# A gated token mixer built from 26-product block schemes: one product as seven sub-products, PSUM in pairs of banks, and another order of the stages

## The chip, the cores and the metric

One Trainium2 chip, one core. The metric is the device time of one execution in microseconds (us); the median of three runs is given. TensorE is called PE, VectorE DVE, ScalarE ACT, GpSimd POOL and SyncE SP. POOL and SP issue the DMAs.

## The reference

All is f32: x is 2048 x 1024 (S x D), the MLP works along S with F = 3584. The Fourier branch is the real part of the two-dimensional DFT, by DFT matrices. The other branch is a layer norm and an MLP across tokens.

```
a = x @ hid_re.T ; b = x @ hid_im.T
y = seq_re @ a - seq_im @ b                  # branch A, S x D
h = layernorm(x)                             # over D
u = gelu(w1.T @ h + b1)                      # F x D
o = w2.T @ u + b2                            # branch B, S x D
g = sigmoid(sum over D of x * gate_w)        # one number per row
out = g * y + (1 - g) * o
```

## The kernel before, in words

There are four matrix products, each a stage (a class derived from `Bilinear`): `Fourier` (q, the sequence DFT of x), `Mixed` (y, the hidden DFT of q), `Up` (u) and `Down` (o). Each stage cuts its two operands into 4 x 4 and 4 x 2 blocks, and computes the block product by a bilinear scheme with 26 block products where the plain way takes 32. An operand of product j is a sum or difference of blocks, made on DVE (`add`, `sub`; L569, L572). It is then split into a high and a low part (`split_into`): ACT writes the high part rounded to fp32r (L599), DVE the remainder (L604, L606). PE multiplies high by high, high by low and low by high (L902, L903, L904), so one 128x128x512 piece is three matmuls. In PSUM the products of the scheme are "chained" where one product can go on accumulating in the banks of the one before. Where results are due, a bank is read (evicted): copied by ACT or DVE (`plain_copy`, L938, L940) or added to a result in SBUF by DVE (`fused`, L946). Down's evictions multiply by the row's gate as well: `hgate`, `ngate` on DVE, or ACT at L1210.

The names: `q_p9` is the tenth product of stage q; `q_R...`, `q_W...` its blocks and their sums; `_r_`, `_w_` with hi and lo the split operands; `ps_o_p9_2_0` the PSUM bank for rows block 2 of o's product 9; `o_c...` a result of Down that is being summed in SBUF. `Q_TAKES = 1, 1, 2` says how many blocks of K the groups of a product take: PE works through all banks of one group before the next group.

SBUF and PSUM are divided into fixed slots: `SLOTS` has 51 full tiles of 1024 columns, and 8 PSUM tiles `ps` of one bank (512 columns). A half buffer takes half of a full tile.

No queue decides at run time. `Graph.schedule` is a list scheduler: each instruction has a cost and a due time from its `key` (a place in PE's sequence), and is written out, engine by engine, in the order that results. On each engine that order is fixed, and semaphores hold an instruction back until what it reads or overwrites is ready. PE's order is that of the stages and products.

Of the kernel before, what the change touches and what calls it, by code (L numbers as in the profile page):

```python
# [14 lines left out]
P = 128  # L15
# [3 lines left out]
H = 512  # L19
# [5 lines left out]
SLOTS = {"f": 51, "h": 1, "ps": 8}  # L25
LATE = 3.0

# [112 lines left out]
Q_GAP = 8  # L140
U_ORDER = [20, 9, 8, 19, 15, 18, 1, 16, 10, 4, 21, 22, 11, 7, 3, 17, 5, 14, 23, 6, 24, 0, 13, 12, 2, 25]
# [68 lines left out]
SUMS_AT, SUMS_STEP = ("q", 12), 2.5  # L210
SQUARES_AT, SQUARES_STEP = ("y", 6), 2
H_LEAD, H_EACH = 25, 1.3
# [49 lines left out]
class Buf:  # L262
    def __init__(self, kind, name, t=None, parts=1, dtype=F32):
        self.kind, self.name, self.t, self.parts, self.dtype = kind, name, t, parts, dtype
        self.writer = [None] * parts
        self.readers = [[] for _ in range(parts)]
        self.taker = None
        self.users, self.opens = set(), False


class View:
# [7 lines left out]
    @property  # L279
    def reg(self):  # L280
        return (self.buf, self.part)

# [19 lines left out]
class Store:  # L302


    def __init__(self, slots):
        self.free = {k: [Slot(k, i) for i in range(n)] for k, n in slots.items()}
        self.part = {F32: [], F32R: []}

    def pairs(self, ahead):
        return sum((max(0, ahead[d] - len(self.part[d])) + 1) // 2 for d in self.part)  # L310

    def fits(self, b, ahead):
        if b.kind != "h":
            return len(self.free[b.kind]) > ahead[b.kind]
        if len(self.part[b.dtype]) > ahead[b.dtype]:
            return True
        return len(self.free["f"]) + len(self.free["h"]) > ahead["f"] + self.pairs(ahead)

    def take(self, b):
        if b.kind != "h":  # L320
            b.slot = min(self.free[b.kind], key=lambda s: s.at), None
            self.free[b.kind].remove(b.slot[0])
            return
        halves = self.part[b.dtype]
        if halves:
            b.slot = min(halves, key=lambda x: x[0].at)
            halves.remove(b.slot)
        else:
            pool = self.free["h"] or self.free["f"]
            b.slot, b.opens = (min(pool, key=lambda s: s.at), 0), True  # L330
            pool.remove(b.slot[0])
            if b.slot[0].pool == "f":
                halves.append((b.slot[0], 1))
        b.slot[0].inside[b.slot[1]] = True

    def give(self, b, now):
        s, h = b.slot
        s.at = now
        if h is not None and s.pool == "f":
            s.inside[h] = False  # L340
            if s.inside[1 - h]:
                self.part[b.dtype].append(b.slot)
                return
            self.part[b.dtype].remove((s, 1 - h))
        self.free[s.pool].append(s)


class Graph:
# [63 lines left out]
    def schedule(self):  # L412
        store = Store(SLOTS)
        waiting = {k: [] for k in ("f", F32, F32R, "ps")}
# [11 lines left out]
        for t in self.tasks:  # L426
            left[t] = len(t.deps)
            for b in t.bufs:
                users[b] = len(b.users)
            for b in t.need:  # L430
                insort(waiting[b.dtype if b.kind == "h" else b.kind], t)
# [6 lines left out]
        def has_slots(t):  # L438
            if not all(b.engine for b in t.behind):
                return False  # L440
            for b in t.need:
                if not store.fits(b, {k: bisect_left(waiting[k], t) for k in waiting}):
                    return False
            return True

        def start(t, e):
            nonlocal dma
            t.engine, t.start = e, now
            order.append(t)
            for b in t.need:  # L450
                store.take(b)
                waiting[b.dtype if b.kind == "h" else b.kind].remove(t)
# [50 lines left out]
def gated_mix_kernel(  # L503
# [30 lines left out]
        "ps": (ctx.enter_context(tc.tile_pool(name="psum", bufs=1, space=bass.MemoryType.PSUM)), H),  # L534
# [138 lines left out]
    class Bilinear:  # L673
# [10 lines left out]
        behind = ()  # L684
        ahead = 3

        def __init__(self, name, nk, nm, nn, wn, rn, big, keep, order, extra, perm):
# [7 lines left out]
            self.again = {j: s for j in range(1, len(rows)) for s in (1, -1) if small[j] == [s * c for c in small[j - 1]]}  # L695
# [13 lines left out]
            for i, (w, v) in enumerate(zip(self.out, self.out[n:])):  # L709
                same = sum(a != b for a, b in zip(w, v))  # L710
                opposite = sum(a != -b for a, b in zip(w, v))
                go_on = min(same, opposite) < sum(a != 0 for a in w)
# [18 lines left out]
        def groups(self):  # L731
# [14 lines left out]
        def during(self, j, key):  # L746

            if (self.name, j) == SUMS_AT:
# [3 lines left out]
                gates(key + SUMS_STEP * NS)  # L752
            if (self.name, j) == SQUARES_AT:
                for row in range(NS):
                    row_squares(row, key + SQUARES_STEP * row)
                rstds(key + SQUARES_STEP * NS)

# [45 lines left out]
        def operand(self, x, j, k, key):  # L803
# [3 lines left out]
            for o, ((a, ca, la), (b, cb, lb)) in ops:  # L807
                if self.by_dma(x, j, k, o):
                    swap = self.fresh(x, a, k, la) is None
                    if swap:  # L810
                        (a, ca, la), (b, cb, lb) = (b, cb, lb), (a, ca, la)
                    src = self.fresh(x, a, k, la)
                    if src is not None and lb and fresh.get(b) != k and (b >= (16 if x == self.big else 8) or x not in self.resident):
                        held = (b, k) in self.val[x] or b < (16 if x == self.big else 8)
                        sb = self.val[x][b, k][1] if (b, k) in self.val[x] else self.stored.get((x, b, k), 1)
                        if held and ca * src[1] == cb * sb:
# [10 lines left out]
                            continue  # L827
                (va, sa, mine_a), (vb, sb, mine_b) = self.term(x, a, la, j, k, key), self.term(x, b, lb, j, k, key)
# [61 lines left out]
        def matmuls(self, j, ks, ops, eps):  # L890
            first, end = ks[0] == 0 and not self.chained[j], ks[-1] == self.nk - 1
            for m in range(self.nm):
                c = slice(m * P, (m + 1) * P)
                for n in range(self.nn):
                    if first:
                        self.PS[j % self.chains, m, n] = View(Buf("ps", f"ps_{self.name}_p{j}_{m}_{n}", None, 4), 0, H)
# [11 lines left out]
                    if end:  # L908
                        key = step + len(ks) + (m * self.nn + n) / (self.nm * self.nn)
                        for q, coef in self.reads[j]:  # L910
                            b = self.perm[0][q // 2] * 2 + self.perm[2][q % 2]
                            o = self.C.get((b, m, n))
                            back = self.back(b, j)
                            if o is None:
                                o = self.C[b, m, n] = self.c_slots(f"{self.name}_c{b}", b, m, n)
                                if back:
                                    self.bring(key - self.ahead, b, m, n, o)
                                    self.accumulate(key, b, m, n, o, bank, eps * coef)
                                else:
                                    self.copy(key, b, m, n, o, bank, eps * coef)  # L920
                            else:
                                self.accumulate(key, b, m, n, o, bank, eps * coef)
                            if j in self.ends[b]:
                                self.finish(key + 1, b, m, n, self.C.pop((b, m, n)), j)

        def c_slots(self, name, b, m, n):
            i = m * self.nn + n
# [22 lines left out]
    class Fourier(Bilinear):  # L950
        wide = Q_WIDE
        behind = Q_BEHIND
        gap = Q_GAP
# [4 lines left out]

        def source(self, x_, b, k):
# [3 lines left out]
            return x[i * P:(i + 1) * P, h * H:(h + 1) * H], ()  # L963

# [52 lines left out]
        def matmuls(self, j, ks, ops, eps):  # L1017
# [13 lines left out]
            if j or ks != (0,):  # L1031
                return super().matmuls(j, ks, ops, eps)
            for n in range(2):
                for m in range(4):
                    self.PS[0, m, n] = View(Buf("ps", f"ps_q_p0_{m}_{n}"), 0, H)
# [137 lines left out]
    class Down(Bilinear):  # L1173
# [5 lines left out]
        ahead = O_AHEAD  # L1179

# [82 lines left out]
    def row_sums(k, key):  # L1263
# [4 lines left out]
        g.add({"DVE": dve(D)}, key, lambda e: nc.vector.scalar_tensor_tensor(  # L1268
            v.ap, v.ap, 1.0, GW.ap, op0=ALU.mult, op1=ALU.mult, accum_out=zg.t[:, col]),
            r=(v.reg, GW.reg), w=(v.reg, zg))  # L1270

    def small(engine, key, fn, r, w, n=1):
        g.add({engine: 0.2 * n}, key, fn, r=r, w=w)

    def gates(key):
# [6 lines left out]
        def rest(e):  # L1282
# [10 lines left out]
        small("DVE", key, lambda e: nc.vector.tensor_scalar(  # L1293
            nmean.t, sums.t, -1.0 / D, None, op0=ALU.mult), (sums,), (nmean,))
# [34 lines left out]
    def normalise(k, v, key):  # L1329

        load(key, v, x[k * P:(k + 1) * P, :])
        g.add({"ACT": act(D) + 0.08}, key, lambda e: nc.scalar.activation(
# [14 lines left out]
    for st in (Fourier(), Mixed(), Up(), Down()):  # L1347
        st.build()
# [60 lines left out]
```

## Time and profile before

| | |
|---|---|
| timed runs, median of 3 | 1849.24 us (1849.2 to 1850.03) |
| span of the profiled execution | 1847.2 us |
| PE busy, matmuls | 1843.0 us, 8130 |
| DVE busy, instructions | 1692.7 us, 2372 |
| ACT busy, instructions | 876.2 us, 1311 |
| POOL busy | 207.2 us |
| granted TensorE clock | 1.000 |
| DMA | 472.71 MB, mean 256 GB/s |

The profiled execution's own time is its span, from the first instruction to the last; the device time of a run holds about 2 us more. In a group's row stand: line, engine, operation, out<-in, tile shapes, count, then busy time and mean ns of one, then the engine's idle time just ahead of them and what ended it. In a timeline row stand start and duration in us. A PE record is longer than the pitch of the matmuls, since they overlap in the pipeline.

### The profile page before, as it was taken

The page shows a single profiled execution, that of the slowest core. Times are in us where ns is not written, and L with a number is a line of the kernel's source. Part 1 is how long each engine was busy: PE and PEld are TensorE (multiplying, and loading weights), DVE is VectorE, ACT ScalarE, POOL GpSimd, SP SyncE. Part 2 cuts the span into 40 slices and gives each one's busy share as a digit, 9 for nine tenths or more (in the row PEclk, how much of TensorE's full clock was granted, in tenths as well). Part 3 has the DMA queues.
Part 4 walks back from the last instruction along what each step waited for, and adds up shares of the span by engine and source line. Part 5 has one row for each costly group of instructions (what it writes and reads, how often), then busy time and mean ns, then how long its engine had stood idle before and what let it go on. Part 6 is the DMA issues. An engine that isn't in the chain of part 4 may idle for free.

```text
span 1847.2 us, 24030 instructions
## 1 busy us (share of the span) xinstructions
PE 1843.0 (100%) x8130; PEld 1525.2 (83%) x8130; DVE 1692.7 (92%) x2372; ACT 876.2 (47%) x1311; POOL 207.2 (11%) x355
## 2 busy tenths in 40 slices
PE   9999999999999999999999999999999999999999
PEld 7888888888888888888888888888888888888887
DVE  8999679989989999999789698879999999999995
ACT  5533334534344686597343344444654534444441
POOL 0100010111021001001121000001220000001111
PEclk9999999999999999999999999999999999999999
DMA  9977377969698888988676547667899676775963
GB/s 377 368 260 270 126 280 289 349 236 376 237 333 313 303 292 273 332 312 292 219 256 241 174 136 255 225 210 247 301 365 295 193 210 208 217 215 128 301 156 69
DMA packets 189739, 472.71 MB, mean 256 GB/s; under 512 B 23152, under 2 KB 23920, under 8 KB 189616
## 3 DMA queue, kind: packets, MB, share of 16 engines
q1 hardware_dynamic: 156384, 368.40, 58.4%
q0 software_dynamic: 32944, 102.52, 16.6%
q8 instruction: 63, 1.03, 0.2%
q14 instruction: 60, 0.49, 0.1%
q10 hardware_dynamic: 288, 0.26, 0.0%
HBM read 367.29 MB, written 103.81 MB: 255 GB/s over the span
## 4 chain that ended last, share of the span: by engine, by line
PE 100%; DVE 0%; issue 0%; DVEq 0%
PE ps_q_p L902 10%; PE ps_q_p L904 10%; PE ps_q_p L903 10%; PE ps_u_p L904 9%; PE ps_u_p L902 9%; PE ps_u_p L903 9%; PE ps_o_p L902 9%; PE ps_o_p L904 9%; PE ps_o_p L903 9%; PE ps_y_p L903 5%; PE ps_y_p L904 5%; PE ps_y_p L902 5%; PE ps_q_p L1049 0%; PE ps_q_p L1026 0%; PE pw L1343 0%; DVE o_c L946 0%
## 5 line engine op out<-in xcount | busy, mean ns | idle before, releaser
L904 PE MATMUL ps_q_p<-q_p_r_hi,q_p_w_lo 128*128 128x512 f32 x728 | 283.2, 389 | 0.0
L902 PE MATMUL ps_o_p<-o_p_r,o_p_w 128*128 128x512 f32 x726 | 282.4, 389 | 0.0
L903 PE MATMUL ps_o_p<-o_p_r,o_p_w 128*128 128x512 f32 x726 | 282.4, 389 | 0.0
L904 PE MATMUL ps_o_p<-o_p_r,o_p_w 128*128 128x512 f32 x726 | 282.4, 389 | 0.0
L903 PE MATMUL ps_u_p<-u_p_r_lo,u_p_w_hi 128*128 128x512 f32 x588 | 228.7, 389 | 0.0
L902 PE MATMUL ps_q_p<-q_p_r_hi,q_p_w_lo 128*128 128x512 f32 x584 | 227.2, 389 | 0.0
L903 PE MATMUL ps_q_p<-q_p_r_lo,q_p_w_lo 128*128 128x512 f32 x584 | 227.2, 389 | 0.0
L902 PE MATMUL ps_u_p<-u_p_r_lo,u_p_w_hi 128*128 128x512 f32 x504 | 196.1, 389 | 0.0
L904 PE MATMUL ps_u_p<-u_p_r_lo,u_p_w_lo 128*128 128x512 f32 x504 | 196.1, 389 | 0.0
L599 ACT ACTIVATE q_p_r_hi<-q_R_p 128x1024 fp32r<-128x1024 f32 (+1 forms) x100 | 104.2, 1053 | 161.8 <-DVE q_R_p L569 78.7
L599 ACT ACTIVATE u_p_w_hi<-u_W_p 128x896 fp32r<-128x896 f32 x104 | 97.1, 950 | 141.1 <-DVE u_W_p L569 69.5
L904 PEld LDWEIGHTS ps_q_p<-q_p_r_hi,q_p_w_lo 128*128 128x128 f32 x728 | 136.7, 188 | 28.4
L904 PEld LDWEIGHTS ps_o_p<-o_p_r,o_p_w 128*128 128x128 f32 x726 | 136.3, 188 | 28.4
L902 PEld LDWEIGHTS ps_o_p<-o_p_r,o_p_w 128*128 128x128 f32 x726 | 136.3, 188 | 28.2
L903 PEld LDWEIGHTS ps_o_p<-o_p_r,o_p_w 128*128 128x128 f32 x726 | 136.3, 188 | 28.2
L599 ACT ACTIVATE o_p_r<-o_R_p 128x512 fp32r<-128x512 f32 x117 | 72.5, 626 | 120.9 <-PE ps_o_p L904 37.3
L903 PEld LDWEIGHTS ps_u_p<-u_p_r_lo,u_p_w_hi 128*128 128x128 f32 x588 | 110.4, 188 | 23.0
L903 PEld LDWEIGHTS ps_q_p<-q_p_r_lo,q_p_w_lo 128*128 128x128 f32 x584 | 109.6, 188 | 22.7
L902 PEld LDWEIGHTS ps_q_p<-q_p_r_hi,q_p_w_lo 128*128 128x128 f32 x584 | 109.7, 188 | 22.6
L946 DVE SCALAR_TENSOR_TENSOR q_c<-ps_q_p,q_c 128x512 f32<-128x512 f32 x168 | 110.3, 686 | 15.6 <-PE ps_q_p L904 11.5
L606 DVE TENSOR_TENSOR q_p_r_lo<-q_R_p,q_p_r_hi 128x1024 fp32r<-128x1024 f32 (+1 forms) x100 | 120.4, 1215 | 4.5 <-ACT q_p_r_hi L599 4.4
L904 PEld LDWEIGHTS ps_u_p<-u_p_r_lo,u_p_w_lo 128*128 128x128 f32 x504 | 94.6, 188 | 19.6
(322 smaller groups left out, 3989.4 us busy)
## 6 DMA issues: line engine op xcount, KB each, us to landing
q_R_p<-in_ct_dram SPq DMA_DIRECT2D x131, 512.0 KB, 7.5
u_W_p<-in_w_dram SPq DMA_DIRECT2D x120, 448.0 KB, 4.7
o_R_p<-in_w_dram SPq DMA_DIRECT2D x99, 256.0 KB, 4.7
o_R_p<-u SPq DMA_DIRECT2D x83, 256.0 KB, 5.2
q<-q_c POOLq DMA_DIRECT2D x80, 256.0 KB, 6.2
o_W_p<-in_w_dram SPq DMA_DIRECT2D x76, 256.0 KB, 4.9
q_W_p<-in_x_dram SPq DMA_DIRECT2D x75, 256.0 KB, 5.5
u<-u_c POOLq DMA_DIRECT2D x72, 256.0 KB, 4.7
```

The costliest lines, as they stand in the source:

```text
L599: g.add({"ACT": act(v.n)}, key, lambda e: nc.scalar.activation(hi.ap, v.ap, AF.Copy, scale=-1.0 if negate else 1.0), r=(v.reg,), w=(hi.reg,))
L606: nc.vector.tensor_sub(lo.ap, v.ap, hi.ap.bitcast(F32))
L902: nc.tensor.matmul(bank.ap, wh.ap[:, c], rh.ap[:, e], start=a, stop=False, skip_group_check=True)
L903: nc.tensor.matmul(bank.ap, wh.ap[:, c], rl.ap[:, e], start=False, stop=False, skip_group_check=True)
L904: nc.tensor.matmul(bank.ap, wl.ap[:, c], rh.ap[:, e], start=False, stop=b, skip_group_check=True)
L946: lambda e: nc.vector.scalar_tensor_tensor(o.ap, ps.ap, scale, o.ap, op0=ALU.mult, op1=ALU.add),
```

## The change

1. `Q_INNER = (24,)`: the scheme's row 24, which is product 9 of stage q, is done by the new function `strassen`: both operands are halved in K, rows and columns, and seven sub-products of 2 x 2 pieces are made (the variant with sums that are used again). It is 84 matmuls in place of 96. DVE makes the extra sums in SBUF, and in PSUM two sums across banks (`add(step, q12, q21, p5)` and `add(step, q22, q21, p5)`).
2. PSUM: 4 tiles `pp` of two banks take the place of 8 of one. With `together` (q, u, y) two neighbouring banks are one buffer and are evicted by one 1024-wide instruction. Down has `together = False`: its banks are single buffers, each a half of a pair tile.
3. `RESERVE = 7` bounds how many slots the planner keeps back for work that is due earlier.
4. The stages run Fourier, Up, Mixed, Down.
5. The row sums, row squares and gates, that the layer norm and the gate need, come at other places: `SUMS_AT`, `SQUARES_AT`, `GATES_AT`, and the DVE product for the gate moves into `normalise`.
6. Stage q takes K in groups of (2, 2) in place of (1, 1, 2), except in product 0, and W of two blocks of K as one 1024-wide tile.

```diff
-SLOTS = {"f": 51, "h": 1, "ps": 8}
+SLOTS = {"f": 51, "h": 1, "pp": 4}
+RESERVE = 7
+Q_INNER = (24,)
-SUMS_AT, SUMS_STEP = ("q", 12), 2.5
-SQUARES_AT, SQUARES_STEP = ("y", 6), 2
-H_LEAD, H_EACH = 25, 1.3
+SUMS_AT, SUMS_STEP = ("q", 4), 2.5
+SQUARES_AT, SQUARES_STEP = ("q", 12), 2
+GATES_AT = "u", 10
+H_LEAD, H_EACH = 8, 0.6
-Q_TAKES = 1, 1, 2
+Q_TAKES = 2, 2
-Q_WIDE, Y_WIDE, O_WIDE = "", "WR", ""
+Q_WIDE, Y_WIDE, O_WIDE = "W", "WR", ""
...
     def take(self, b):
-        if b.kind != "h":
+        if b.kind in ("f", "pp"):
...
-        halves = self.part[b.dtype]
+        halves = self.part[b.lane]
         if halves:
             b.slot = min(halves, key=lambda x: x[0].at)
             halves.remove(b.slot)
         else:
-            pool = self.free["h"] or self.free["f"]
+            pool = self.free["pp"] if b.kind == "ps" else self.free["h"] or self.free["f"]
...
-                if not store.fits(b, {k: bisect_left(waiting[k], t) for k in waiting}):
+                if not store.fits(b, {k: min(bisect_left(waiting[k], t), RESERVE) for k in waiting}):
...
-                for ks in self.groups():
+                if j in self.inner:
+                    self.strassen(j, factor)
+                    continue
+                for ks in self.groups(j):
...
+        def banks(self, j):
+            every = [(m, n) for n in range(self.nn) for m in range(self.nm)]
+            for i, (m, n) in enumerate(every):
+                name = f"ps_{self.name}_p{j}_{m}_{n}"
+                if not self.together or i == len(every) - 1 and i % 2 == 0:
+                    self.PS[j % self.chains, m, n] = View(Buf("ps", name, None, 4), 0, H)
+                elif i % 2 == 0:
+                    both = Buf("pp", name, None, 2)
+                    self.PS[j % self.chains, m, n] = View(both, 0, H, 0)
+                else:
+                    self.PS[j % self.chains, m, n] = View(both, H, H, 1)
...
+            q11, q12, q21, q22 = quarter(0, 0), quarter(0, 1), quarter(2, 0), quarter(2, 1)
+            products(folded(step, "a11", a(0, 0)), halves(step, "b11", [b(0, 0), b(1, 0)]), 2, 0, True, True)
+            step += 1
+            plain_copy(step, q11, q21, 1.0)
...
+            p5 = slot(D, f"{name}_p5")
+            plain_copy(step, p5, q22, 1.0)
...
+            products(folded(step, "s2", Fold(s)), whole(step, "t2", whole_t), 2, 0, False, True)
+            step += 1
+            add(step, q12, q21, p5)
...
+            products(folded(step, "s3", Fold(s3)), whole(step, "t3", whole_t3), 2, 0, False, True)
+            step += 1
+            add(step, q22, q21, p5)
+            ready(2, 1, step + 1)
...
     class Down(Bilinear):
+        together = False
...
-    for st in (Fourier(), Mixed(), Up(), Down()):
+    for st in (Fourier(), Up(), Mixed(), Down()):
```

What the order of instructions shows of it, at three places. A row has its number on the engine, the line, the operation, out<-in and what it waits for; a tile has the name of the buffer that first took it.

PE where Down's product 8 ends and product 9 begins, before:

```order
6703 L903 MATMUL ps_o_p_3_0_12211<-o_p_r_12433,o_p_w_12483 128x512
6704 L904 MATMUL ps_o_p_3_0_12211<-o_p_r_12433,o_p_w_12483 128x512
6705 L902 MATMUL ps_o_p_0_0_12650<-o_p_r_12523,o_p_w_12459 128x512 [waits Activation_49]
6706 L903 MATMUL ps_o_p_0_0_12650<-o_p_r_12523,o_p_w_12459 128x512 [waits DVE_49]
6707 L904 MATMUL ps_o_p_0_0_12650<-o_p_r_12523,o_p_w_12459 128x512
```

And now, PE and then DVE at the same place:

```order
6670 L950 MATMUL ps_o_p_2_0_11851<-o_p_r_12058,o_p_w_12072 128x512
6671 L948 MATMUL ps_o_p_2_0_11851<-o_p_r_12095,o_p_w_12083 128x512 [waits DVE_49,Activation_49]
6672 L949 MATMUL ps_o_p_2_0_11851<-o_p_r_12095,o_p_w_12083 128x512
6673 L950 MATMUL ps_o_p_2_0_11851<-o_p_r_12095,o_p_w_12083 128x512
6674 L948 MATMUL ps_o_p_2_0_11851<-o_p_r_12109,o_p_w_12112 128x512 [waits Activation_49]
6675 L949 MATMUL ps_o_p_2_0_11851<-o_p_r_12109,o_p_w_12112 128x512
6676 L950 MATMUL ps_o_p_2_0_11851<-o_p_r_12109,o_p_w_12112 128x512
6677 L948 MATMUL ps_o_p_2_0_11851<-o_p_r_12095,o_p_w_12083 128x512 [waits DVE_49]
```

```order
1595 L609 TENSOR_TENSOR o_W_p_3_10674<-o_W_p_3_10674 128x512 [waits DMAHW5_49,DMAHW4_49]
1596 L1016 SCALAR_TENSOR_TENSOR o_c_2_11993<-ps_o_p_2_0_11851,ngate,o_c_2_11993 128x512 [waits PE_49]
1597 L606 TENSOR_TENSOR o_W_p_2_10641<-o_W_p_3_10674,o_W_p_2_10641 128x512 [waits DVE_49]
1598 L1016 SCALAR_TENSOR_TENSOR o_c_2_11993<-ps_o_p_2_0_11851,ngate,o_c_2_11993 128x512 [waits DMAHW6_49,PE_49]
1599 L643 TENSOR_TENSOR o_p_r_12307<-u_c_6_7355,o_p_r_12307 128x512 [waits Activation_49]
```

Before, product 9 began in a bank of its own (`..._12650`) while product 8's last bank (`..._12211`) was emptied. Now the first matmul of product 9 (row 6671) writes into the tile that product 8's last matmul (row 6670) wrote into, and it waits for DVE, whose evictions of the two halves (rows 1596 and 1598) wait for PE. The second half's first matmul is row 6677.

DVE at the start, behind product 0's operands, before:

```order
12 L569 TENSOR_TENSOR q_R_p_0_277<-q_R_p_0_277,q_R_p_0_286 128x1024 [waits DMAHW4_49,DMAHW3_49]
13 L569 TENSOR_TENSOR q_R_p_0_259<-q_R_p_0_277,q_R_p_0_259 128x1024 [waits DVE_49]
14 L572 TENSOR_TENSOR q_W_p_0_311<-q_W_p_3_273,q_W_p_0_311 128x512 [waits DMAHW6_49,DMAHW5_49]
15 L940 TENSOR_SCALAR q_c_0_410<-ps_q_p_0_0_282 128x512 [waits PE_49]
16 L569 TENSOR_TENSOR q_W_p_0_257<-q_W_p_0_311,q_W_p_0_257 128x512 [waits DVE_49]
17 L606 TENSOR_TENSOR q_p_r_lo<-q_R_p_0_259,q_p_r_hi 128x1024 [waits Activation_49]
18 L569 TENSOR_TENSOR q_R_p_1_315<-q_R_p_1_315,q_R_p_1_333 128x1024 [waits DMAHW7_49,DMAHW0_49]
19 L604 SCALAR_TENSOR_TENSOR q_p_w_lo<-q_W_p_0_257,q_p_w_hi 128x512 [waits Activation_49]
```

And now:

```order
11 L606 TENSOR_TENSOR q_R_p_0_265<-q_R_p_0_265,q_R_p_0_273 128x1024 [waits DMAHW4_49,DMAHW3_49]
12 L606 TENSOR_TENSOR q_R_p_0_247<-q_R_p_0_265,q_R_p_0_247 128x1024 [waits DVE_49]
13 L606 TENSOR_TENSOR q_R_p_1_279<-q_R_p_1_279,q_R_p_1_298 128x1024 [waits DMAHW6_49,DMAHW5_49]
14 L643 TENSOR_TENSOR q_p_r_lo<-q_R_p_0_247,q_p_r_hi 128x1024 [waits Activation_49]
15 L606 TENSOR_TENSOR q_R_p_1_252<-q_R_p_1_279,q_R_p_1_252 128x1024 [waits DVE_49]
16 L609 TENSOR_TENSOR q_W_p_0_1_329<-q_W_p_0_1_302,q_W_p_0_1_329 128x1024 [waits DMAHW2_49,DMAHW7_49,DMAHW1_49,DMAHW0_49]
17 L643 TENSOR_TENSOR q_p_w_1_lo<-q_W_p_0_1_302,q_p_w_1_hi 128x1024 [waits Activation_49]
18 L606 TENSOR_TENSOR q_W_p_0_1_344<-q_W_p_0_1_329,q_W_p_0_1_344 128x1024 [waits DMAHW4_49,DMAHW3_49,DVE_49]
19 L643 TENSOR_TENSOR q_p_r_lo<-q_R_p_1_252,q_p_r_hi 128x1024 [waits Activation_49]
20 L606 TENSOR_TENSOR q_R_p_2_367<-q_R_p_2_367,q_R_p_2_371 128x1024 [waits DMAHW6_49,DMAHW5_49]
21 L641 SCALAR_TENSOR_TENSOR q_p_w_1_lo<-q_W_p_0_1_344,q_p_w_1_hi 128x1024 [waits Activation_49]
```

The first group of product 1 had its W part ready with row 19, after one block of K; now with row 21, after two, and W is summed and split 1024 columns at a time.

DVE in the last part of q's product 9, now:

```order
169 L1010 TENSOR_SCALAR q_p_p_1836<-ps_q_p_2_1_1807 128x1024 [waits DVE_49,PE_49]
170 L643 TENSOR_TENSOR q_p_t_lo<-q_p_t,q_p_t_hi 128x1024 [waits Activation_49]
171 L609 TENSOR_TENSOR q_W_p_0_1_1740<-q_W_p_0_1_1740,q_W_p_0_1_1791 128x1024 [waits DMAHW6_49,DMAHW5_49,DMAHW3_49]
172 L606 TENSOR_TENSOR ps_q_p_0_1_1860<-ps_q_p_2_0_1780,q_p_p_1836 128x1024 [waits DVE_49,PE_49]
173 L643 TENSOR_TENSOR q_p_r_lo<-q_R_p_0_1718,q_p_r_hi 128x1024 [waits Activation_49]
174 L1016 SCALAR_TENSOR_TENSOR q_c_0_761<-ps_q_p_0_0_1814,q_c_0_761 128x1024 [waits PE_49]
175 L643 TENSOR_TENSOR q_p_w_1_lo<-q_W_p_0_1_1740,q_p_w_1_hi 128x1024 [waits Activation_49]
176 L643 TENSOR_TENSOR q_p_r_lo<-q_R_p_1_1772,q_p_r_hi 128x1024 [waits Activation_49]
177 L606 TENSOR_TENSOR ps_q_p_2_1_1807<-ps_q_p_2_0_1780,q_p_p_1836 128x1024 [waits PE_49]
```

Rows 172 and 177 are the two sums in PSUM. Before, product 9 had no such rows: only its low parts and eight evictions of 512 columns.

More of the change, by code (lines that the diff above doesn't have):

```diff
@@ L684, in gated_mix_kernel @@
         behind = ()
+        halved = ()
+        together = True
         ahead = 3
@@ L694, in __init__ @@
             small = [r[1] for r in rows]
-            self.again = {j: s for j in range(1, len(rows)) for s in (1, -1) if small[j] == [s * c for c in small[j - 1]]}
+            self.inner = [j for j, r in enumerate(order) if r in self.halved]
+            self.again = {j: s for j in range(1, len(rows)) for s in (1, -1)
+                          if small[j] == [s * c for c in small[j - 1]] and not {j, j - 1} & {*self.inner}}
             self.kept = {}
@@ L711, in __init__ @@
                 opposite = sum(a != -b for a, b in zip(w, v))
-                go_on = min(same, opposite) < sum(a != 0 for a in w)
+                go_on = min(same, opposite) < sum(a != 0 for a in w) and i + n not in self.inner
                 self.chained.append(go_on)
@@ L908, in matmuls @@
                     if end:
[L909 to L924, printed above, removed]
+                        self.take(step + len(ks) + (n * self.nm + m) / (self.nm * self.nn), j, m, n, eps)
@@ new lines, in take @@
+        def take(self, key, j, m, n, eps):
+            bank, at = self.PS[j % self.chains, m, n], [(m, n)]
+            if bank.buf.kind == "pp":
+                if bank.c0 == 0:
+                    return
+                at.insert(0, (m - 1, n))
+                bank = View(bank.buf, 0, D)
+            for q, coef in self.reads[j]:
+                b = self.perm[0][q // 2] * 2 + self.perm[2][q % 2]
+                new, back = (b, m, n) not in self.C, self.back(b, j)
+                if new:
+                    for one in at:
+                        self.C[(b, *one)] = self.c_slots(f"{self.name}_c{b}", b, *one)
+                os = [self.C[(b, *one)] for one in at]
+                o = os[0] if len(at) == 1 else View(os[0].buf, 0, D)
+                if new and back:
+                    for one, part in zip(at, os):
+                        self.bring(key - self.ahead, b, *one, part)
+                if new and not back:
+                    self.copy(key, b, m, n, o, bank, eps * coef)
+                else:
+                    self.accumulate(key, b, m, n, o, bank, eps * coef)
+                if j in self.ends[b]:
+                    for one in at:
+                        self.finish(key + 1, b, *one, self.C.pop((b, *one)), j)
```

178 lines of the change are left out of this document (144 added, 34 removed).

## The prediction

> **What bounds the kernel now.** I read the page first (busy times, clock, chain), then the waits of PE, then single instructions.
>
> ```profile
> PE 1843.0 (100%) x8130; PEld 1525.2 (83%) x8130; DVE 1692.7 (92%) x2372; ACT 876.2 (47%) x1311; POOL 207.2 (11%) x355
> PEclk9999999999999999999999999999999999999999
> q1 hardware_dynamic: 156384, 368.40, 58.4%
> q0 software_dynamic: 32944, 102.52, 16.6%
> PE 100%; DVE 0%; issue 0%; DVEq 0%
> PE pw L1343 <- PEq L1396: 0.8, 1, 0.8
> ```
>
> PE is busy for 1843.0 of 1847.2 us at a full granted clock, the chain is PE, and the last row is the whole answer on PE's waits: one start of 0.8 us. Once running, PE never waits. So the time is the number of matmuls times their pitch, 1843.0 / 8130 = 0.2267 us. The profiled span is 1847.2 us; the median of the timed runs is 1849.24, so 2.0 us lie around the span, and I carry them unchanged.
>
> The second question is who could make PE wait. By stretches of 50 us (the columns are PE, PEld, DVE, ACT and POOL busy, then granted clock, DMA share and GB/s):
>
> ```profile
> 0.00:50.00 50.00, 49.22 (x212) 39.36 (x213) 41.92 (x50) 28.08 (x41) 0.20 (x4) 1.00 0.99 380
> 200.00:250.00 50.00, 50.00 (x222) 41.44 (x221) 37.54 (x47) 18.72 (x27) 0.82 (x2) 1.00 0.49 164
> 1400.00:1450.00 50.00, 50.00 (x222) 41.41 (x221) 50.00 (x83) 21.08 (x37) 0.86 (x1) 1.00 0.79 255
> 1500.00:1550.00 50.00, 50.00 (x223) 41.40 (x222) 50.00 (x84) 21.18 (x37) 4.71 (x8) 1.00 0.67 210
> ```
>
> DVE is full in Down (the two rows from 1400 us) and three quarters full around the tenth q product (200 us). PE is full beside it only because every bank that it writes was emptied early. The prices of emptying a bank:
>
> ```profile
> L946 DVE SCALAR_TENSOR_TENSOR o_c<-ps_o_p,ngate,o_c 128x512 f32<-128x512 f32 x52 | 38.8, 747 | 15.6 <-PE ps_o_p L904 15.4
> L1210 ACT ACTIVATE o_c<-ps_o_p,hgate 128x512 f32<-128x512 f32 x14 | 9.5, 687 | 10.3 <-PE ps_o_p L904 10.3
> 1839.20 0.39 PE L904 MATMUL ps_o_p<-o_p_r,o_p_w 128*128 128x512 f32 x1
> 1839.62 0.75 DVE L946 SCALAR_TENSOR_TENSOR o_c<-ps_o_p,ngate,o_c 128x512 f32<-128x512 f32 x1 [13.55 <-PE ps_o_p L904]
> 3.59 0.42 ACT L993 ACTIVATE q_p_w_hi<-q_W_p 128x256 fp32r<-128x256 f32 x1 [0.64 <-DMA q_W_p<-in_x_dram]
> 4.05 1.14 PEld L1049 LDWEIGHTS ps_q_p<-q_p_r_hi,q_p_w_hi 128*128 128x128 f32 x5 [0.61 <-ACT q_p_w_hi L993]
> 4.06 1.22 PE L1049 MATMUL ps_q_p<-q_p_r_hi,q_p_w_hi 128*128 128x256 f32 x4
> ```
>
> An eviction takes 0.75 us on DVE, 0.69 on ACT. A matmul's record is 0.39 long, so it ends 0.16 after the next one could start (0.39 - 0.23). From that end to the eviction's start: 1839.62 - 1839.59 = 0.03 us. From an operand's end to PE's restart: 4.06 - 4.01 = 0.05.
>
> **The change part by part.**
>
> *Seven sub-products.* The tenth q product falls from 96 to 84 matmuls, the program from 8130 to 8118. On PE's path: -12 x 0.2267 = -2.72 us. Its cost is on DVE: 19 instructions of 512 columns and 9 of 1024 for sums, low parts, copies and PSUM adds, 28 where a plain product has 6 or so. The spare time is in the row at 200 us (DVE 37.54 of 50). Two PSUM adds stand between a sub-product and the next but one, whose first matmul waits for them: the chain is 0.19 + up to two 1024-wide instructions, and the 12 matmuls between take 2.72 us:
>
> ```profile
> L569 DVE TENSOR_TENSOR q_R_p<-q_R_p,q_R_p 128x1024 f32<-128x1024 f32 x84 | 100.8, 1220 | 1.3 <-DMA q_R_p<-in_ct_dram 0.8 <-DMA q_R_p<-q_R 0.4
> 14.99 2.48 DVE L569 TENSOR_TENSOR q_R_p<-q_R_p,q_R_p 128x1024 f32<-128x1024 f32 x2 [0.50 <-DMA q_R_p<-in_ct_dram]
> 15.67 0.39 PE L902 MATMUL ps_q_p<-q_p_r_hi,q_p_w_hi 128*128 128x512 f32 x1
> 26.74 3.49 DVE L569 TENSOR_TENSOR q_R_p<-q_R_p,q_R_p 128x1024 f32<-128x1024 f32 x3
> ```
>
> One takes 1.22 us, and in the last row three start (3.49 - 1.22) / 2 = 1.14 apart. 0.19 + 1.14 + 1.22 + 0.05 = 2.60, so 0.12 is left of 2.72. A PSUM add reads and writes PSUM, which no row shows; with the 1.22 of the 1024-wide SBUF form I charge 0.3 for the block, 0 to 2 in the range.
>
> *Start-up.* Product 1 begins 48 matmuls after the PE row above: 15.67 + 10.88 = 26.55. Before, its first group took one block of K. Now it takes two, with W as one 1024-wide tile. From the DMA-bound DVE row at 14.99 on, the order has eleven 1024-wide instructions up to and including W's low part: 14.99 + 10 x 1.14 + 1.22 = 27.61, needed by the third matmul at 27.00. Cost 0.65, with 0.3 and 2 as ends (DMA is at 0.99 there). A like spot at q product 13: 0.2.
>
> *Down's banks.* Here lies the sum. PSUM tiles are now pairs of banks. Down still takes single banks (`together` is False), as halves of a pair tile. Two things follow in the order shown above. A product that isn't chained takes the half bank just finished, where before it took a fresh bank. And the program's eviction of one half waits for the semaphore count of the last matmul into the tile, the other half's included. At o_p9, the eviction of the first half of `ps_o_p_2_0_11851` waits for the last matmul of o_p8, and the next matmul on PE waits for that eviction: no work lies between them. Six matmuls later the same happens with the other half, whose eviction waits for those six. PE stops twice per product for 0.16 + 0.03 + eviction + 0.05:
> - one DVE eviction: 0.99. o_p9 twice, o_p15 twice, o_p16 once: 4.95
> - one ACT eviction: 0.93. o_p3 twice: 1.86
> - ACT's, then DVE's on the same bank (0.69 + 0.03 + 0.75): 1.71. o_p6 and o_p12 twice each: 6.84
>
> Together 13.65 us. No cover can hide it, since the eviction cannot start before PE's last matmul nor PE go on before its end. Bounds for one stop: the eviction alone, 0.69 or 0.75 (sum 10.8), and 0.19 more for a weight load that could not go ahead, or one DVE instruction of 0.69 already under way ahead of it (sum 16 to 22).
>
> Where Down's products are chained, a pair tile is free for 12 matmuls, 2.72 us, and four DVE evictions run in it. Starts of neighbours here lie 0.67 apart:
>
> ```profile
> 1516.93 0.74 DVE L946 SCALAR_TENSOR_TENSOR o_c<-ps_o_p,ngate,o_c 128x512 f32<-128x512 f32 x1
> 1517.60 0.68 DVE L572 TENSOR_TENSOR o_W_p<-o_W_p,o_R_p 128x512 f32<-128x512 f32 x1
> ```
>
> 0.19 + 3 x 0.67 + 0.74 + 0.05 = 2.99, 0.27 late; with ACT's in the mix 0.1. Nine such places: 1.7 us, 0 to 4.
>
> *Pairs in q, y, u.* One 1024-wide eviction replaces two of 512:
>
> ```profile
> L946 DVE SCALAR_TENSOR_TENSOR q_c<-ps_q_p,q_c 128x512 f32<-128x512 f32 x168 | 110.3, 686 | 15.6 <-PE ps_q_p L904 11.5 <-ACT q_c L938 3.5
> ```
>
> It saves 2 x 0.69 - 1.22 = 0.15 each on DVE, which isn't the path. Price: the pair waits for both banks. In y, two evictions of a pair need 2.60 of 2.72 us, and DVE is over-full there: the order gives y 349 DVE instructions, 288 us by the rows' pitches, against 283 us of matmuls. The backlog reaches about 1.5 us late; once PE has stopped that long the later waits are met. Cost 1.5, 0 to 11 (the 11 products that are late, each by up to 1).
>
> *Stage order, RESERVE, the moved row sums and squares, wider W blocks:* DMA bytes (368 MB on SP's queue, 102 on POOL's) and ACT's work (47% busy) are nearly unchanged (369 and 102 MB, and ACT 1160 instructions in place of 1311, more of them 1024 wide), the z sums only move on DVE, from q to ahead of Up. Nothing beyond the backlogs above; -1 to +3.
>
> Sum: -2.72 + 0.3 + 0.85 + 13.65 + 1.7 + 1.5 = +15.3. Span 1862.5, time 1864.5 us.
>
> [...]
>
> **The rivals.**
> - *Not slower: the stops vanish.* If an eviction in Down were released by its own bank's last matmul, it would have 6 matmuls, 1.36 us, ahead of PE's need, and 0.99 fits. Time 1864.5 - 13.65 = 1850.9, the same within what a measurement can tell; without the y and chain terms also, 1849.24 - 2.72 = 1846.5. It decides from 12 us of vanished stops on. Against it: the counts in the built program. Chance 0.06 for the first, 0.04 for the second, which lies so near 1845.5 that half of it goes to faster.
> - *Backlogs repeat.* Each late y product costs anew, since its evictions wait for PE too: +11 in place of 1.5, 1874; with DVE instructions ahead of Down's evictions 1880. For it: DVE at 50.00 of 50 us. Against: in y the loop closes with 0.12 to spare. Chance 0.13.
> - *The clock falls.* Twelve or so stops come in pairs within 3 to 5 us. [...] Every row has granted clock 1.00, with no stop to test it. Chance 0.07. [...]
>
> **How the numbers follow.** The likeliest, 0.70: the stops as counted, 1864.5, own range 1858 (evictions alone, no y term) to 1870. The range 1857 to 1876 takes in the clock rival and the smaller repeat; about 0.2 is outside. 0.2% is 3.7 us, about what a measurement tells from no change: faster below 1845.5 takes 0.02, the same (to 1852.9) 0.08, slower 0.90.
>
> **What would show it.** The waits of PE, one row before, list Down's banks behind L1016 (DVE) and Down's copy (ACT), 12 to 14 us in some 13 long stops, at most 1.8 us each. The window of o_p6 and o_p12 shows PE short by 3.4 us each, that of y by 1 to 3. PE has 8118 matmuls at the same pitch. A granted clock below 1.00 in Down speaks for the clock rival, y stops over 5 us for the backlog. I am wrong if Down's stops are below 8 us or above 20.

## The result, and the profile after

The changed kernel takes 1871.8 us (median of 4, 1871.47 to 1872.07) against 1849.63 for the kernel before, run beside it: ratio 1.0119, 95% interval 1.0105 to 1.0134. It is slower by 22 us, where the text on record said 15 (1864.5 us, 1857 to 1876). The profiled span grew from 1847.2 to 1869.7 us. (The kernel before was run beside every experiment as well: 1849.4 to 1849.6, so the times below can be compared.)

The page of the changed kernel: busy times, clock, and the chain that ended last.

```profile
PE 1848.6 (99%) x8118; PEld 1519.9 (81%) x8118; DVE 1688.5 (90%) x2091; ACT 873.4 (47%) x1210; POOL 200.7 (11%) x346
PEclk9999999999999999999999999999999999999999
PE 86%; DVE 8%; DMA 3%; issue 1%; ACT 1%; SPq 0%; DVEq 0%; ACTq 0%
```

PE has 12 matmuls fewer and the same clock, and yet the chain runs through DVE for 8%. (Busy PE grew from 1843.0 to 1848.6 us although it did less: a record is 0.39 us long where the pitch is 0.227, and one that comes after a stop, like that of 1533.00 in the timeline below, no longer overlaps the one ahead of it, which ended at 1532.16; so busy time is not the measure here.) In the changed kernel's lines L948, L949 and L950 are the three matmuls, L1016 the eviction that adds, L1403 and L1405 Down's copies, L641 and L643 the low parts. The waits of PE, one row before, are now:

```profile
PE ps_o_p L948 <- DVE o_c L1016: 11.3, 11, 1.7
PE ps_o_p L948 <- ACT o_c L1403: 1.6, 2, 0.8
PE ps_y_p L948 <- DVE y_c L1016: 1.4, 3, 0.6
PE pw L1539 <- PEq L1592: 0.8, 1, 0.8
PE ps_q_p L950 <- DVE q_p_w_lo L641: 0.8, 1, 0.8
PE ps_o_p L948 <- DVE o_c L1405: 0.4, 1, 0.4
```

Down's PSUM banks wait for Down's evictions (L1016 on DVE, L1403 on ACT): 13.3 us in 14 stops, the longest 1.7. Behind it stand y with 1.4, and the start of the program and q's product 1 with 0.8 each. These rows count only the time in which no matmul's record is open; each stop loses more, as the second stop of Down's product 9 shows, in the timeline:

```profile
1531.77 0.39 PE L950 MATMUL ps_o_p<-o_p_r,o_p_w 128*128 128x512 f32 x1
1532.19 0.75 DVE L1016 SCALAR_TENSOR_TENSOR o_c<-ps_o_p,ngate,o_c 128x512 f32<-128x512 f32 x1 [1.19 <-PE ps_o_p L950]
1532.99 0.19 PEld L948 LDWEIGHTS ps_o_p<-o_p_r,o_p_w 128*128 128x128 f32 x1 [1.27 <-DVE o_c L1016]
1533.00 0.50 PE L948 MATMUL ps_o_p<-o_p_r,o_p_w 128*128 128x512 f32 x1 [0.84 <-DVE o_c L1016]
1533.33 0.40 PE L949 MATMUL ps_o_p<-o_p_r,o_p_w 128*128 128x512 f32 x1
```

PE's matmul ends at 1532.16, the eviction runs from 1532.19 to 1532.94, PE starts again at 1533.00. Nothing lies between the three: DVE had been idle for 1.19 us, waiting for that matmul. From start to start it is 1.23 us where 0.227 is the pitch, 1.00 lost; and the matmul after that comes 0.33 later, not 0.227, another 0.11.

The longest stops are those of products 6 and 12, where ACT and then DVE read the same bank. The second one of product 6:

```profile
1471.05 0.40 PE L950 MATMUL ps_o_p<-o_p_r,o_p_w 128*128 128x512 f32 x1
1471.48 0.69 ACT L1403 ACTIVATE o_c<-ps_o_p,hgate 128x512 f32<-128x512 f32 x1 [2.58 <-PE ps_o_p L950]
1472.20 0.75 DVE L1016 SCALAR_TENSOR_TENSOR o_c<-ps_o_p,ngate,o_c 128x512 f32<-128x512 f32 x1 [1.87 <-ACT o_c L1403]
1473.01 0.50 PE L948 MATMUL ps_o_p<-o_p_r,o_p_w 128*128 128x512 f32 x1 [1.57 <-DVE o_c L1016]
```

Here PE's starts are 1.96 us apart, 1.74 lost, and 0.11 more at the next matmul.

I summed by how much each start of a matmul lies further behind the start ahead of it than the pitch, by stage, in this trace against that of before. This is the "lost" time below:

| stage | lost, us | where |
|---|---|---|
| q | 1.7 | 1.04 at product 1, 0.39 at product 13, small rests |
| u | 0.0 | |
| y | 3.4 | five stops of 0.2 to 0.77, 2.3 together; the late second matmuls behind them and small rests |
| o | 19.0 | the eleven stops at unchained products 15.4, the rest at chained ones |
| after the last matmul | 1.1 | evictions 0.65, the last store 0.45 |
| 12 matmuls fewer | -2.7 | |
| sum | 22.5 | the span grew by 22.5 |

By stretches (PE, PEld, DVE, ACT, POOL busy, granted clock, DMA share, GB/s): around the seven sub-products, in y, and two of Down.

```profile
200.00:220.00 20.00, 20.00 (x90) 16.57 (x89) 16.07 (x15) 11.90 (x15) 0.53 (x1) 1.00 0.78 264
1170.00:1220.00 50.00, 48.83 (x213) 39.50 (x212) 48.40 (x58) 20.51 (x28) 4.86 (x9) 1.00 0.62 204
1450.00:1500.00 50.00, 46.57 (x203) 37.51 (x203) 46.39 (x76) 19.35 (x34) 1.73 (x2) 1.00 0.58 181
1500.00:1550.00 50.00, 48.22 (x212) 39.32 (x211) 47.46 (x78) 19.72 (x34) 4.70 (x8) 1.00 0.68 215
```

In the first row PE is full: the block of sub-products has no stop. In the third and fourth, both in Down, DVE has 3.6 and 2.5 us without work and PE loses time as well: they wait for each other.

### The profile page after: what moved, and what is told of

Its sections match the earlier page's. It is cut to its first block, busy times and chain, and to the rows that moved or that the text cites. A ratio compares the mean times of both kernels' runs of the same rounds, so it can differ in the third digit from the quotient of the medians.

```text
span 1869.7 us, 23585 instructions
## 1 busy us (share of the span) xinstructions
PE 1848.6 (99%) x8118; PEld 1519.9 (81%) x8118; DVE 1688.5 (90%) x2091; ACT 873.4 (47%) x1210; POOL 200.7 (11%) x346
## 4 chain that ended last, share of the span: by engine, by line
PE 86%; DVE 8%; DMA 3%; issue 1%; ACT 1%; SPq 0%; DVEq 0%; ACTq 0%
PE ps_o_p L948 9%; PE ps_u_p L949 9%; PE ps_u_p L948 9%; PE ps_u_p L950 9%; PE ps_q_p L950 9%; PE ps_q_p L948 9%; PE ps_q_p L949 9%; PE ps_o_p L950 9%; PE ps_o_p L949 9%; PE ps_y_p L948 2%; PE ps_y_p L950 2%; PE ps_y_p L949 2%; DVE y_c L1016 1%; PE ps_q_p L1097 1%; DVE o_c L1016 1%
## 5 line engine op out<-in xcount | busy, mean ns | idle before, releaser
L950 PE MATMUL ps_q_p<-q_p_r_hi,q_p_w_lo 128*128 128x512 f32 x784 | 305.2, 389 | 0.9 <-DVE q_p_w_lo L641 0.8
L949 PE MATMUL ps_q_p<-q_p_r_lo,q_p_w_hi 128*128 128x512 f32 x784 | 305.0, 389 | 0.0
L948 PE MATMUL ps_q_p<-q_p_r_hi,q_p_w_hi 128*128 128x512 f32 x784 | 305.0, 389 | 0.0
L948 PE MATMUL ps_o_p<-o_p_r,o_p_w 128*128 128x512 f32 x726 | 284.7, 392 | 13.3 <-DVE o_c L1016 11.3
L949 PE MATMUL ps_o_p<-o_p_r,o_p_w 128*128 128x512 f32 x726 | 282.6, 389 | 0.0
L950 PE MATMUL ps_o_p<-o_p_r,o_p_w 128*128 128x512 f32 x726 | 282.6, 389 | 0.0
L949 PE MATMUL ps_u_p<-u_p_r_lo,u_p_w_hi 128*128 128x512 f32 x518 | 201.5, 389 | 0.0
L948 PEld LDWEIGHTS ps_o_p<-o_p_r,o_p_w 128*128 128x128 f32 x726 | 136.2, 188 | 49.3 <-DVE o_c L1016 13.1
L950 PEld LDWEIGHTS ps_q_p<-q_p_r_hi,q_p_w_lo 128*128 128x128 f32 x784 | 147.1, 188 | 32.4 <-DVE q_p_w_lo L641 1.7
L949 PEld LDWEIGHTS ps_q_p<-q_p_r_lo,q_p_w_hi 128*128 128x128 f32 x784 | 147.1, 188 | 30.7
L948 PEld LDWEIGHTS ps_q_p<-q_p_r_hi,q_p_w_hi 128*128 128x128 f32 x784 | 147.2, 188 | 30.2
L950 PEld LDWEIGHTS ps_o_p<-o_p_r,o_p_w 128*128 128x128 f32 x726 | 136.3, 188 | 28.5
L949 PEld LDWEIGHTS ps_o_p<-o_p_r,o_p_w 128*128 128x128 f32 x726 | 136.3, 188 | 27.7
L948 PE MATMUL ps_u_p<-u_p_r_hi,u_p_w_hi 128*128 128x512 f32 x385 | 149.8, 389 | 0.0
L950 PE MATMUL ps_u_p<-u_p_r_hi,u_p_w_lo 128*128 128x512 f32 x385 | 149.8, 389 | 0.0
L948 PE MATMUL ps_u_p<-u_p_r_lo,u_p_w_hi 128*128 128x512 f32 x343 | 133.4, 389 | 0.0
L950 PE MATMUL ps_u_p<-u_p_r_lo,u_p_w_lo 128*128 128x512 f32 x343 | 133.4, 389 | 0.0
L643 DVE TENSOR_TENSOR q_p_r_lo<-q_R_p,q_p_r_hi 128x1024 fp32r<-128x1024 f32 (+1 forms) x96 | 115.5, 1217 | 9.6 <-ACT q_p_r_hi L636 5.9
L1016 DVE SCALAR_TENSOR_TENSOR q_c<-ps_q_p,q_c 128x1024 f32<-128x1024 f32 x84 | 101.1, 1222 | 23.1 <-PE ps_q_p L950 20.2
L949 PEld LDWEIGHTS ps_u_p<-u_p_r_lo,u_p_w_hi 128*128 128x128 f32 x518 | 97.2, 188 | 20.2
```

Of the source, the lines that this page charges most:

```text
L643: nc.vector.tensor_sub(lo.ap, v.ap, hi.ap.bitcast(F32))
L948: nc.tensor.matmul(bank.ap, wh.ap[:, c], rh.ap[:, e], start=a, stop=False, skip_group_check=True)
L949: nc.tensor.matmul(bank.ap, wh.ap[:, c], rl.ap[:, e], start=False, stop=False, skip_group_check=True)
L950: nc.tensor.matmul(bank.ap, wl.ap[:, c], rh.ap[:, e], start=False, stop=b, skip_group_check=True)
L1016: lambda e: nc.vector.scalar_tensor_tensor(o.ap, ps.ap, scale, o.ap, op0=ALU.mult, op1=ALU.add),
```

## The experiments

Theory A: PE stops because two banks share a tile, so that an eviction waits for the matmuls of the other half, and because an unchained product of Down begins in just that tile. Theory B: DVE has too much to do in the new order of stages, and PE would wait whatever the bank.

**e1, another choice of pair.** DVE, ACT and PE do the same instructions in the same order as in the changed kernel; in Down other banks are used.

```diff
         halves = self.part[b.lane]
-        if halves:
+        if b.kind == "ps" and self.free["pp"] and halves and min(s.at for s in self.free["pp"]) < min(x[0].at for x in halves):
+            b.slot, b.opens = (min(self.free["pp"], key=lambda s: s.at), 0), True
+            self.free["pp"].remove(b.slot[0])
+            halves.append((b.slot[0], 1))
+        elif halves:
```

> Changed kernel with one edit: a product of Down that opens new banks takes the pair that has been free longest, not a half that is just being emptied. All else of the order is the same. Theory A (PE stops in Down because the next product starts in the tile whose eviction waits for PE's last matmul): the stops at Down's products 3, 6, 9, 12, 15 and 16, 15.4 us with the restart, fall away, the short ones where products are chained stay and grow by up to 1 us: 1857 us (1855 to 1860), PE waits on Down's banks under 4 us. Theory B (DVE is over-full in Down, so PE waits for evictions whatever bank it takes): the waits move to other places, 1866 us or more.

Measured: 1858.52 us (1857.38 to 1860.02), ratio to before 1.0048 (1.0034 to 1.0062). PE's waits but for the start:

```profile
PE ps_q_p L954 <- DVE q_p_w_lo L645: 3.3, 2, 1.7
PE ps_o_p L952 <- DVE o_c L1020: 1.7, 3, 1.3
PE ps_y_p L952 <- DVE y_c L1020: 1.5, 3, 0.6
PE ps_o_p L952 <- DVE o_c L1409: 0.4, 1, 0.4
```

Down's waits fall from 13.3 to 2.1 us and the time by 13.3, with the same work on DVE in the same order. Theory B asked for 1866 or more. The same sum of starts gives 5.3 us lost in o where it was 19.0. All of it stands at chained products, which grew by 1.7 from 3.6, more than the 1 that was allowed: product 7 now loses 1.5 by itself, where it lost 0.4 (the stops of product 6 just ahead probably gave DVE time, which was not tried). In the profiled run q's products 1 and 13 cost 3.8 and not 1.4: at product 13 DVE sat idle for 1.40 us, waiting for a transfer of x, so the start and product 13 vary from run to run.

**e2, without the seven sub-products.** `Q_INNER = ()`.

> Changed kernel with the tenth q product as one plain product (12 matmuls more); the stages behind q have the same order. If the seven sub-products are hidden on DVE as reckoned: 2.7 us slower than the changed kernel, 1874.5 us (1873.9 to 1875), 8130 matmuls. If the block's sums cost PE as much as it saves: 1871.8, no change. If the block is what made the kernel slow: well below 1871.

Measured: 1874.9 us (1874.33 to 1875.77), 3.1 slower than the changed kernel; the stops behind q are the same ones, to about 0.02 us each. So the block is worth about its 12 matmuls and is not what made the kernel slow. One stop does go with it: the one at q's product 13 (0.39 in the changed kernel) stands in the traces of all six kernels with the block, and in none of those without it (before, e2, e6, e8). Which of the rows that the planner moved for the block makes it was not tried.

**e3, Down with a tile for each bank.**

```diff
+SLOTS = {..., "pp": 4, "p1": 8}
     class Down(Bilinear):
         together = False
+        bank_kind = "p1"
...
+            if s.pool == "p1" and "p1" not in pools:
+                first.close()
+                pools["p1"] = (ctx.enter_context(tc.tile_pool(name="psum1", bufs=1, space=bass.MemoryType.PSUM)), H)
```

> Changed kernel in which Down has eight PSUM tiles of one bank each, as in the kernel before, opened when the last pair of y is free; q, u and y keep pairs. Theory A, in the form that the tile of two banks is what ties an eviction to the other half: the stops of Down's products 3 to 16 fall away, 15.4, and also those of the chained products, 3; the handover between stages may cost up to 3: 1854 to 1858 us. Theory B: 1866 us or more.

Measured: 1853.39 us (1853.22 to 1854.37), ratio 1.0022 (1.0013 to 1.0031), 0.6 under the range, which had left out 0.65 us at the end of the program (below). All its waits of PE but the start:

```profile
PE ps_y_p L957 <- DVE y_c L1025: 1.4, 3, 0.6
PE ps_o_p L957 <- DVE y_c L1025: 1.3, 1, 1.3
PE ps_q_p L959 <- DVE q_p_w_lo L649: 0.2, 1, 0.2
```

No stop is left in Down behind its first matmul, which waits for y's last eviction (1.3, the handover of PSUM). The chained products' stops have gone too. And DVE is as full as ever there:

```profile
1500.00:1550.00 50.00, 50.00 (x222) 41.40 (x221) 50.00 (x83) 20.42 (x36) 4.70 (x8) 1.00 0.64 196
```

DVE 50.00 of 50 beside a PE of 50.00: a full DVE does not stop PE here. In e3 the planner also put some of Down's rows on DVE in another order; in e1 it did not. The two together leave the shared tile as the cause, and Theory B falls for Down.

**e4, less work for DVE in y.** In y the sums made in place write 64 columns:

```diff
+        n = 64 if part else o.n
+        cut = (lambda v: v.ap[:, :n]) if part else (lambda v: v.ap)
...
+                (add if ca * sa == cb * sb else sub)(key, v, va, vb, self.name == "y" and v in (va, vb))
```

> Changed kernel in which stage y's sums of blocks that are made in place write 64 columns only (123 DVE instructions; the sums are left unfinished), in the same order. If y's 3.4 us of lost pitch are DVE's backlog: they fall to under 0.5, and Down's first products gain up to 1 too: 1867.5 us (1867 to 1868.6). If they come from the 12 matmuls between a pair's end and its next use: 1871 us or more.

Measured: 1870.28 us (1869.57 to 1871.11), 1.5 faster; y's lost pitch falls from 3.4 to 1.9.

```profile
1170.00:1220.00 50.00, 49.33 (x217) 40.34 (x216) 36.90 (x60) 22.16 (x31) 5.38 (x10) 1.00 0.64 219
1300.00:1350.00 50.00, 49.62 (x219) 40.60 (x218) 43.48 (x60) 28.83 (x46) 11.46 (x22) 1.00 0.87 290
```

DVE is down to 36.90 and 43.48 of 50 here and PE still stops, for 0.83 us at 1199.01 and 0.54 at 1338.54. So neither expectation held: the sums that were cut short make about half of y's loss. Down's first products gained nothing: Down still loses 19.0. The two stops that stay have different causes. At the first one, ACT and DVE:

```profile
1195.26 1.52 ACT L1311 ACTIVATE y_c<-y_c,biases,gate 128x512 f32<-128x512 f32 x2 [1.29 <-DVE y_c L1020]
1196.69 1.01 ACT L1012 ACTIVATE y_c<-ps_y_p 128x1024 f32<-128x1024 f32 x1
1197.73 1.22 DVE L1020 SCALAR_TENSOR_TENSOR y_c<-ps_y_p,y_c 128x1024 f32<-128x1024 f32 x1 [1.24 <-ACT y_c L1012]
```

By the order of the matmuls the pair's last one ended at 1195.63 (1195.24 + 0.39). ACT copied the pair only from 1196.69 on, behind two rows that apply the gate, and DVE, whose eviction waits for that copy, sat idle for 1.24 us until it was done. So the chain here runs through ACT's order of rows and not through DVE's backlog. (In the changed kernel the stop at the same place, 0.77, looks the same: DVE idle for 0.76 behind ACT's copy.) At the second stop it is backlog still: DVE runs without a pause from 1324.2 us on, and three evictions stand one behind the other:

```profile
1336.04 3.48 DVE L1020 SCALAR_TENSOR_TENSOR y_c<-ps_y_p,y_c 128x1024 f32<-128x1024 f32 x3
```

**e5, one-bank tiles from u on.** As e3, for u, y and o, with a pool for each pair of q and for each bank behind it, so that a bank waits for the pair that lay there alone. With the pairs go the wide evictions of u and y: they are 512 columns wide again (2220 instructions on DVE where the changed kernel has 2091).

> Changed kernel in which u, y and o all have eight PSUM tiles of one bank, and only q has pairs; each pair of q is a pool of its own, so that a bank of u is tied to the pair that lay there and not to all four. Theory A (all lost pitch behind q comes from the pair tiles): PE waits in q alone, 1 to 3 us at products 1 and 13, none in u, y and o: 1847 to 1849.5 us, at or under the kernel before. Rival (y's and Down's loss is DVE's backlog from the new order of stages): 2 us or more of waits stay in y and o, 1850 us or more.

Measured: 1848.61 us (1847.79 to 1849.58), ratio 0.9995 (0.9986 to 1.0004): the same as before. The whole answer on PE's waits, and the stretch of y:

```profile
PE ps_q_p L960 <- DVE q_p_w_lo L650: 1.0, 1, 1.0
PE pw L1553 <- PEq L1611: 0.8, 1, 0.8
1170.00:1220.00 50.00, 50.00 (x223) 41.40 (x222) 49.88 (x71) 24.33 (x35) 4.32 (x8) 1.00 0.57 194
```

y's loss is gone with DVE at 49.88 of 50, at the changed kernel's order of stages. The rival of 1850 and more does not hold. Whether the single tiles or the narrower evictions that come with them save y, e5 can't tell apart.

**e6, e5 without the sub-products; e8, with q's groups of K as before as well** (`Q_TAKES = 1, 1, 2`, `Q_WIDE = ""`).

> The kernel of e5 with the tenth q product as one plain product. If the seven sub-products are worth their 12 matmuls: 2.7 us slower than e5, so 1850 to 1852 us; if not, the same as e5.

> The kernel of e6 (no sub-products, one-bank tiles from u on) with q's groups of K and narrow W as in the kernel before (1, 1, 2). If the stop at product 1 comes from the wider first group: no stop there, 1.3 to 2.4 us faster than e6, 1849 to 1850 us, level with the kernel before. If it comes from something else in q (pairs of banks, the order of the sums): 1851.3 as e6.

Measured: e6 1851.27 us (1850.66 to 1853.16), 2.66 more than e5, where 12 pitches are 2.72. e8 1849.64 us (1849.36 to 1850.93), 1.63 less than e6, ratio to before 1.0002 (0.9993 to 1.0011). In e8 the only wait of PE is the one of the kernel before:

```profile
PE pw L1553 <- PEq L1611: 0.8, 1, 0.8
```

So the wider groups of K, with the wide W (put back together, not one by one), make the loss at q's product 1; that of product 13 is gone in e6 already. The order of stages, the moved sums, `RESERVE` and q's own pairs together cost nothing that can be seen. The 1.63 is not to be read too closely: in e6's profiled run, the longest of its runs, PE also waited 0.8 us for an operand of product 0.

**e7, a row moved at the start of e5.** A dependence given to the planner alone puts product 1's W low part ahead of a sum for its next group.

```diff
+                late = (self.lo1,) if self.name == "q" and j == 1 and x == "R" and k in (2, 3) else ()
```

> The kernel of e5 with one DVE row moved at the start: product 1's W low part goes ahead of a sum that only the next group of K needs. In e5 ACT's high part ended at 25.87 us and DVE began the low part at 26.73, with that sum in between. If the start-up stop (1.24 us with its restart) is DVE's order, it falls by 0.8: 1847.8 us. If it is the transfers' time, no change: 1848.6.

Measured: 1847.85 us (1847.68 to 1848.5), ratio 0.9992 (0.9983 to 1.0000), 0.76 less than e5, where 0.8 was expected, though the two intervals overlap. In the profiled runs the wait fell from 1.0 to 0.5 us. DVE's rows at the place, in e7:

```profile
24.44 1.22 DVE L615 TENSOR_TENSOR q_W_p<-q_W_p,q_W_p 128x1024 f32<-128x1024 f32 x1
25.57 1.22 DVE L652 TENSOR_TENSOR q_p_r_lo<-q_R_p,q_p_r_hi 128x1024 fp32r<-128x1024 f32 x1
26.79 1.23 DVE L650 SCALAR_TENSOR_TENSOR q_p_w_lo<-q_W_p,q_p_w_hi 128x1024 fp32r<-128x1024 f32 x1
```

In that run the first sum that waits for a transfer began at 16.19 us, in e5 at 15.07. W's low part then began 10.60 us behind it (26.79), where in e5 it was 11.66 (26.73). So the moved row gave about one row's time, and the half that is left of the wait goes, in this run, with the transfers. It is the fastest version of all, 0.08% under the kernel before, which lies at the edge of its interval.

## Why the prediction was right, and where its sum was short

- **Seven sub-products, -2.72 + 0.3.** Right in the gain: e6 less e5 is 2.66. Inside the block the 0.3 for the PSUM sums was too much: PE has no stop between 200 and 220 us, and a sum that reads and writes PSUM takes 1.23 us, where the SBUF form takes 1.22. The first of the two, in the changed kernel:

```profile
211.00 1.23 DVE L606 TENSOR_TENSOR ps_q_p<-ps_q_p,q_p_p 128x1024 f32<-128x1024 f32 x1
```

  What the block does cost stands later, in the stop of product 13 (0.39; see e2), which the text counted with the start-up as 0.2.
- **Down's unchained products, 13.65.** Right in place, mechanism and number of stops: e1 takes away just the choice of bank and with it 13.3 us of time. Each stop was mis-sized. It lost 1.05 (ACT), 1.11 or 1.18 (DVE) and 1.84 to 1.94 (ACT, then DVE), where the text had 0.93, 0.99 and 1.71: 15.4 in all. The term that was short is the restart. The text took 0.05 us for it, from one restart at the program's start; the slower restart (0.19 for a weight load) stood there as the upper bound. Of the 1.7 us that were missing, 1.1 is the late matmul behind the first (0.08 to 0.11 at each of the eleven stops), for which the text had nothing. The other 0.6 lies in the hops between engines, up to 0.12 at the first stop of a product: at product 9's first stop PE starts 0.15 behind the eviction's end (1530.55 behind 1530.40), at its second 0.06 (1533.00 behind 1532.94).
- **Chained products, 1.7.** They and small rests lost 3.6. The gap of 12 matmuls with four evictions was the right place (e3 brings them to nothing); each of the nine also pays the 0.08 to 0.11.
- **y, 1.5.** Lost 3.4. The step that failed is "once PE has stopped that long the later waits are met": it took the two evictions of a pair as fitting (2.60 of 2.72 us) and the loss from DVE's work over the whole stage, and had no term for an eviction that starts late. e4 shows that the work is about half of the loss. Of what stays, one stop is ACT's copy that came late behind other rows of ACT, the other DVE's rows in series. All of it goes when the pairs go (e5).
- **Start-up and product 13, 0.85.** Lost 1.7 here; the stops at those two places took 0.8 (e3) to 3.8 us (e1) from run to run. The step had the start as DVE's eleven rows at their pitch. The first of them waits for a transfer, and began at 15.26 in the profiled run, not at 14.99; W's low part ended at 28.13, not at 27.61. Within the range that was given for it (0.3 to 2) in this run, beyond it in e1.
- **The end of the program, not in the sum.** 1.1 us, of which 0.65 is DVE's end after the last matmul's start: 1.59 us, where before and e5 have 0.94. So it goes with the pairs too; that it is the half-width bank of the last block, which shares a tile, fits and was not tried. The other 0.45 lies in the last store and was not followed.
- **Stage order, RESERVE, moved sums: nothing.** Right, by e8.
- **The signs.** The waits of PE came as said: 13.3 us in 14 stops, the longest 1.7. Products 6 and 12 are short by 3.8 and 3.7 where 3.4 was said, y by 3.4 where it was 1 to 3.

The terms that were missed all lie on the same side, so the sum was short by 7 us: 1.7 in the stops of unchained products, 1.9 in the chained ones, 1.9 in y, 0.9 in q, 1.1 at the end, less 0.3 for the block.

Of the rivals, the stops that vanish did not come: the program's counts hold on the chip, with 13.3 us of waits in Down. With a tile for each bank the evictions run beside matmuls into other banks, and PE does not stop: between 1500 and 1550 us DVE and PE are both at 50.00 of 50 us, in e3 and in e5. The backlogs repeated in part (y, where 3.4 us were lost and not 11). The clock did not fall under the matmuls: the granted clock is 1.00 from 1450 to 1500 and from 1580 to 1630 us, where two stops of 1.8 to 1.9 us, 3.2 us apart, stand at each of products 6 and 12. Over the run its mean is 1.000; the one lower value lies behind the last matmul, which ended at 1865.14: 0.55 from 1869.00 to 1869.70 us. The range of 1857 to 1876 took the clock rival in. No run shows what a lower clock costs the matmuls, so that part of the range was the author's estimate; what the runs showed is 22 us more at a clock of 1.00.

## What to carry to other kernels

Here a buffer of two banks tied the reader of one half to the writer of the other, since the program's dependences go by tile: PE waited for 13.3 us in Down, and behind Down's first matmul not at all with a tile for each bank (e3). Before widening buffers to halve the count of evictions, look for the place where the next product starts in the tile just finished: there the distance between writer and reader is zero, and spare time on DVE did not hide it: DVE had been idle for 1.19 us ahead of the eviction at 1532.19, and PE stopped all the same. A share of busy time does not tell it: with single banks DVE at 50.00 of 50 us stopped nothing (e3), and with pairs PE still stopped in a stretch where DVE was busy for 36.90 (e4). There the trace had to be followed row by row, and it led to ACT.

## What the runs showed of the hardware

Behind each stop of 0.15 us and more in the changed kernel's q, y and Down, from 10 us on, the second matmul comes 0.31 to 0.34 us behind the first and not 0.227. The first one's record is 0.47 or 0.50 long in place of 0.39, and the next weight load (1533.10 in the timeline of the changed kernel, 0.19 long) starts 0.08 to 0.11 behind the first matmul's start, here 0.10 behind 1533.00:

```profile
1533.10 0.19 PEld L949 LDWEIGHTS ps_o_p<-o_p_r,o_p_w 128*128 128x128 f32 x1
```

Behind the matmuls that follow without a stop it is 0.00 to 0.01 nearly everywhere, as at 1531.32 behind 1531.31. So each of these stops costs 0.08 to 0.11 us more than its wait; that the late weight load is the cause fits the row, and was not tried by itself. At four chained products, where the stop itself is 0.15, this adds 0.11.
